# Attention heads of the last two batches spread in one stream over the mixture's second and third batch of columns and seven output tiles

## The chip, the cores and the metric

One core of a Trainium2 chip runs the whole program. The metric is device time in microseconds (us), the median of three runs. TensorE does the matmuls and transposes, VectorE (DVE), ScalarE (ACT) and GpSimd (POOL) do the elementwise work, SyncE (SP) issues the DMA transfers.

## The reference

Attention over 4 batches, 12 heads, 448 positions and 64 channels feeds a mixture of three products with a maximum over them, and that feeds eight experts of which each token takes one:

```python
scores = scale * np.matmul(q, k.transpose(0, 1, 3, 2))
scores = np.where(mask, -1000000000.0, scores)      # causal
attn = exp(scores - max); attn /= sum
x = np.matmul(attn, v)                              # (1792, 768) once the heads stand side by side
h = np.maximum(np.maximum(x @ w1, x @ w2), x @ w3)  # (1792, 768)
y = h @ w_out                                       # (1792, 768)
e_idx = np.argmax(y @ w_gate, axis=1)
...
out[mask] = gate_w * eom * (np.maximum(y[mask] @ e_w1[e], 0) @ e_w2[e])
```

## The kernel before

A unit u is a pair of heads of one batch: 24 units, six for each batch, so batch 2 is units 12 to 17 and batch 3 units 18 to 23. Units 0 to 11 are worked in an order written out by hand, beside the mixture of batch 0. From there on the order is made by three generators and by `mix` (L806), and each engine takes its instructions in that order nearly as they are written.

- `attn_stream` (L564) yields the work of units 12 to 23 in 85 steps, seven to a unit: scores (`at_qk`, L433: 24 matmuls into six PSUM banks, named ss), two steps of transposes of the other head of the unit before (`at_p`, L497: three banks pp, 10 transposes), its product with v (`at_av`, L525: 8 matmuls into av) with the transposes pr of the row sums, the transposes of this unit's first head in two steps, the second with the transposes pq and pk of the next unit's q and k (`at_t`, L407), and the product av of the first head. ps_t (L96) has six PSUM banks, which all of these share with the transposes pwt of w_out. VectorE takes scores out of their banks with one instruction for each block (L466), ScalarE does the exponentials (L471).
- `h_stream(b)` (L691) yields the mixture of batch b in 36 halves of 9 matmuls (L674). Two halves make one product in one bank pm of the two banks of psm (L85). `h_max` (L678) copies the first of three products to g on ScalarE, takes the maximum with the second and third on VectorE (L685), and writes hth (ScalarE, L688) and htl (VectorE, L689). The weights wp come back from memory in 384 KB pieces, five tiles ahead (L657).
- `y_half(t, a)` (L707) yields one half of the columns of output tile t in two steps of 9 matmuls (L713) into a psm bank py, and ends with a copy ys (ScalarE, L722). Tiles 0 to 6 read the hth and htl of batches 0 and 1, so they stand after `h_stream(1)`; `h_stream(2)` writes over batch 0's place in them, so it stands after tile 6.
- `wo_stream` (L207) unpacks w_out beside `h_stream(1)` in 12 pieces: ScalarE L159 and L160, VectorE L165 to L167 and GpSimd L170 make a piece wor, ScalarE and GpSimd split it, TensorE transposes it (pwt, L194), and for each second piece TensorE multiplies it with the gates (pg, L200: 6 matmuls in the program, two passes of each in the trace, into a psm bank).
- `x_split(hp)` (L612) writes the parts xh (ScalarE, L615) and xl (L617, VectorE for odd hp, GpSimd for even) of the finished heads xf. There is one buffer each of xf, xh and xl for a pair of heads, so the split of batch 2 must come after the last half of `h_stream(1)` that reads batch 1's, and batch 3's heads write xf only after that split.

`mix` walks one generator and after each of its steps adds `ratio` to a counter that stands for head steps, at most 1.0 of which is carried:

```python
for _ in st:
    next(beside, None)
    acc[0] += ratio
    while acc[0] >= 1.0 and not all(u in done for u in range(NN, upto)):
        next(ast, None)
        acc[0] -= 1.0
    acc[0] = min(acc[0], 1.0)
```

Before, 36 halves of `h_stream(1)` take 1.33 head steps each, which is 47 steps and finishes batch 2; all six splits follow; the 28 steps of tiles 0 to 6 take 1.75 each, so the last 38 steps of heads are used up before tile 6; `h_stream(2)` (L830) then runs with nothing beside it. After it come the splits of batch 3, tiles 7 to 9, the routing, `h_stream(3)` and the experts.

Of the kernel before, what the change touches and what calls it, by code (L numbers as in the profile page):

```python
# [23 lines left out]
def f32(ap):  # L24
    return ap.bitcast(F32)
# [7 lines left out]
def kernel(  # L33
# [18 lines left out]
    NP = H // 2  # L52
# [17 lines left out]


    G_PRIO = 300
    RATIO = (1.33, 1.75)
    WB = 5
    DA, SA = 6, 3

# [3 lines left out]
    def prio(n):  # L80
        return tc.high_priority(offset=n)
# [34 lines left out]
    def wo_tiles(dt, name):  # L116
        for a in "hl":
            wo[a] = wo_p.tile([P, KF, DM + 2 * E], dt, tag="wo" + a, name=name + a)
# [12 lines left out]
    def drain(g):  # L131
        for _ in g:
            pass
# [4 lines left out]
    def decode_load(src, n=0):  # L138
        n = n % 6
        if n < 2:  # L140
            raw = dec.tile([P, 2 * HC], I32, tag="raw", name="raw")
        else:
            raw = wo["h"][:, n - 2, : 2 * HC]
        raw = raw.rearrange("p (n t) -> p n t", t=2)
        if len(src.shape) == 2:
            dst = raw.rearrange("p n t -> p (n t)")
        else:
            dst = raw.rearrange("p (k n) t -> p k (n t)", k=src.shape[1])
        nc.sync.dma_start(out=dst, in_=src)
        return raw  # L150

    def decode_act(raw, n=0):
        lo, hi = raw[:, :, 0], raw[:, :, 1]
        if n % 3:
            tlf = wo["l"][:, n % 3 - 1, : 2 * HC]
        else:
            tlf = dec.tile([P, 2 * HC], I32, tag="tlf", name="tlf", bufs=1)
        t, lf = tlf[:, :HC].bitcast(F32), tlf[:, HC : 2 * HC]
        nc.scalar.activation(t, hi.bitcast(F32), AF.Abs, scale=65536.0)  # L159
        nc.scalar.activation(lf, lo.bitcast(U32), AF.Copy, scale=2.0**-29)  # L160
        return t, lf

    def decode_steps(dst, raw, t, lf):
        hi, ti = raw[:, :, 1], t.bitcast(I32)
        yield nc.vector.tensor_scalar(out=t, in0=t, scalar1=LO, scalar2=HI, op0=ALU.max, op1=ALU.min)  # L165
        yield nc.vector.tensor_single_scalar(ti, ti, 3, op=ALU.logical_shift_left)
        yield nc.vector.scalar_tensor_tensor(  # L167
            out=ti, in0=hi, scalar=-0x80000000, in1=ti, op0=ALU.bitwise_and, op1=ALU.bitwise_or
        )
        nc.gpsimd.tensor_tensor(out=dst.bitcast(I32), in0=ti, in1=lf, op=ALU.add)  # L170
# [12 lines left out]
    def wo_src(f, a):  # L183
        return w_out[f * P : (f + 1) * P, 2 * HC * a : 2 * HC * (a + 1)]

    def wo_split(f, a, wr):
        yc = slice(HNL * a, HNL * a + HN)
        nc.scalar.copy(wo["h"][:, f, yc], wr)
        nc.gpsimd.tensor_sub(wo["l"][:, f, yc], wr, f32(wo["h"][:, f, yc]))

    def wo_t(f, a, wr, wt):
        pt = ps_t.tile([P, 512], F32, tag="pst", name=f"pwt{f}_{a}")
        for c in range(3):
            nc.tensor.transpose(pt[:, c * P : (c + 1) * P], wr[:, c * P : (c + 1) * P], ident)  # L194
        nc.vector.tensor_copy(wt[:, 3 * a : 3 * a + 3, :], pt[:, : 3 * P])

    def wo_g(f, wt):
        pg = psm.tile([P, 512], F32, tag="mm", name=f"pg{f}")
        for dk in range(KD):
            nc.tensor.matmul(  # L200
                pg[:, : 2 * E], lhsT=wt[:, dk, :], rhs=wg[:, dk].rearrange("p a e -> p (a e)"),
                start=dk == 0, stop=dk == KD - 1,
            )
        nc.scalar.copy(wo["h"][:, f, HN:HNL], pg[:, : 2 * E])
        nc.vector.tensor_sub(wo["l"][:, f, HN:HNL], pg[:, : 2 * E], f32(wo["h"][:, f, HN:HNL]))

    def wo_stream():  # L207
        wo_tiles(F32R, "wo")
        raw = decode_load(wo_src(0, 0))
        for n in range(2 * KF):  # L210
            f, a = divmod(n, 2)
            if a == 0:
                wt = dec.tile([P, KD, P], F32, tag="wt", name=f"wt{f}", bufs=1)
            wr = dec.tile([P, HC], F32, tag="wraw", name=f"wor{n}", bufs=3)
            steps = decode_steps(wr, raw, *decode_act(raw))
            if n + 1 < 2 * KF:
                raw = decode_load(wo_src(*divmod(n + 1, 2)))
            drain(steps)
            yield
            wo_split(f, a, wr)  # L220
            wo_t(f, a, wr, wt)
            yield
            if a:
                wo_g(f, wt)
                yield
# [6 lines left out]
    NN, NU = 2 * NP, B * NP  # L232
    raws, done = {}, set()
# [378 lines left out]
    def x_split(hp):  # L612
        xh = xtp.tile([P, S], F32R, tag=f"xh{hp}", name=f"xh{hp}")
        xl = xtp.tile([P, S], F32R, tag=f"xl{hp}", name=f"xl{hp}")
        nc.scalar.copy(xh, xf[hp])  # L615
        eng = nc.vector if hp % 2 else nc.gpsimd
        eng.tensor_sub(xl, xf[hp], f32(xh))  # L617
        xs[hp] = (xh, xl)
# [38 lines left out]
    def ahead(n):  # L657
        while fetched[0] < min(n, len(seq)):
            b, i, a = seq[fetched[0]]
            wp = wst.tile([P, 2, 3, P], F32R, tag="wp", name=f"wp{b}_{i}_{a}", bufs=WB)  # L660
            nc.sync.dma_start(out=f32(wp).rearrange("p a k n -> p (a k n)"), in_=wpdram[2 * i + a])
            wtiles[b, i, a] = wp
            fetched[0] += 1
# [3 lines left out]
    def h_half(b, i, a):  # L667
        pm = gs["pm", b, i] = gs.get(("pm", b, i)) or psm.tile([P, 512], F32, tag="mm", name=f"pm{b}_{i}")
        wp = wtiles.pop((b, i, a))
        for kk in range(3 * a, 3 * a + 3):  # L670
            xh, xl = xs[kk]
            wh, wl = wp[:, 0], wp[:, 1]
            for c, (l, r) in enumerate(((wh, xh), (wh, xl), (wl, xh))):
                nc.tensor.matmul(  # L674
                    pm[:, :S], lhsT=l[:, kk % 3, :], rhs=r, start=kk == 0 and c == 0, stop=kk == KD - 1 and c == 2
                )
# [14 lines left out]
    def h_stream(b):  # L691
        for i in range(NCH):
            n = NH * (b - 1) + 2 * i
            ahead(n + WB)
            h_half(b, i, 0)
            ahead(n + 1 + WB)
            yield
            h_half(b, i, 1)
            with prio(G_PRIO):
                h_max(b, i)  # L700
            yield


    def y_cols(t):
        return slice(P * (t % 7), P * (t % 7) + P)

    def y_half(t, a):  # L707
        cs = y_cols(t)
        c0, w = (0, HNL) if a == 0 else (HNL, HN)
        pm = psm.tile([P, 512], F32, tag="mm", name=f"py{t}_{a}")  # L710
        for kk in range(KF):
            for c, (l, r) in enumerate(((hth, wo["h"]), (htl, wo["h"]), (hth, wo["l"]))):
                nc.tensor.matmul(  # L713
                    pm[:, :w], lhsT=l[:, kk, cs], rhs=r[:, kk, c0 : c0 + w], start=kk == 0 and c == 0,
                    stop=kk == KF - 1 and c == 2,
                )
            if kk == 2:
                yield
        if a == 0:
            nc.vector.tensor_copy(lg[:, t].rearrange("p a e -> p (a e)"), pm[:, HN:HNL])  # L720
        ys = ysp.tile([P, HN], F32, tag="ys", name=f"ys{t}_{a}")
        nc.scalar.copy(ys, pm[:, :HN])  # L722
        nc.sync.dma_start(out=ydram[t * P : (t + 1) * P, HN * a : HN * a + HN], in_=ys)
        yield
# [81 lines left out]
    def mix(st, upto, ratio, beside=iter(()), acc=[0.0]):  # L806
# [8 lines that stand above are left out]
    def rest(upto):  # L815
        while not all(u in done for u in range(NN, upto)):
            next(ast)

    wos = wo_stream()
    mix(h_stream(1), NP * 3, RATIO[0], wos)  # L820
    rest(NP * 3)
    for hp in range(NP):
        x_split(hp)
    drain(wos)
    for t in range(7):
        for a in range(2):
            mix(y_half(t, a), NU, RATIO[1])
    rest(NU)
    ph_a.close()
    for _ in h_stream(2):  # L830
        pass
    for hp in range(NP):
        x_split(hp)
    for t in range(7, 10):
# [153 lines left out]
    rest = rt.tile([P, E], F32, name="rest")  # L988
# [343 lines left out]
```

## Time and profile before

| | |
|---|---|
| median of 3 runs | 963.58 us (962.23 to 967.49) |
| the profiled execution | 967.17 us, of which 965.4 us are the span from its first to its last instruction |
| TensorE busy | 931.5 us, 96% of the span |
| VectorE, ScalarE, GpSimd busy | 484.1, 456.1 and 167.3 us |
| chain of work that ended last | TensorE 80%, VectorE 8%, ScalarE 5%, issue 3%, DMA 3% |

The profile is one execution. A matmul's busy time overlaps that of the next, so TensorE's progress is read from start to start, and its losses from the idle time that the trace puts before an instruction together with what ended it. PEld is TensorE's weight load, which runs beside the matmuls. In the rows, SPq is the queue of SyncE.

### The profile page before, as it was taken

Reading aid. Unit: us, or ns where it says so; the run is one execution under the profiler, and the core shown is the slowest. Engines: PE = TensorE matmul, PEld = TensorE weight load, DVE = VectorE, ACT = ScalarE, POOL = GpSimd, SP = SyncE. Lnnn points to the kernel's source line nnn. Section 1 sums busy time; section 2 is a strip of 40 time slices with the busy share of each in tenths; the row PEclk is TensorE's granted clock in tenths of the full one; section 3 lists DMA queues with packets and bytes.
Section 4 is the critical chain, followed back from the end, with each engine's and each line's share of the span. In section 5 each row is a group of like instructions: output and inputs, shape, how many; then the busy total and the mean of one; then the engine's idle time right before and its main releaser. Section 6 shows DMA issues by size and latency. Waiting matters only on the chain.

```text
span 965.4 us, 17091 instructions
## 1 busy us (share of the span) xinstructions
PE 931.5 (96%) x5500; PEld 825.5 (86%) x5500; DVE 484.1 (50%) x1287; ACT 456.1 (47%) x1037; POOL 167.3 (17%) x186
## 2 busy tenths in 40 slices
PE   8888999999999999999999999899999999999997
PEld 5666888888889989989999899888998998998996
DVE  4665777867776666662124313641211217749244
ACT  5876676655666567761012013142212216757253
POOL 0114555542221121010001000010010010100101
PEclk9998999999999999999999999999999999999999
DMA  6436878876564542204772994181111016939410
GB/s 144 101 92 200 250 247 242 255 241 186 154 167 128 144 131 68 59 26 147 218 213 86 329 332 125 52 325 54 34 44 56 34 38 228 357 128 370 155 34 26
DMA packets 126354, 150.10 MB, mean 155 GB/s; under 512 B 75934, under 2 KB 93342, under 8 KB 126240
## 3 DMA queue, kind: packets, MB, share of 16 engines
q1 hardware_dynamic: 123200, 135.37, 44.8%
q0 software_dynamic: 3040, 13.41, 4.0%
q8 instruction: 46, 0.75, 0.3%
q14 instruction: 68, 0.56, 0.2%
HBM read 129.85 MB, written 26.77 MB: 162 GB/s over the span
## 4 chain that ended last, share of the span: by engine, by line
PE 80%; DVE 8%; ACT 5%; issue 3%; DMA 3%; POOL 1%; SPq 0%; POOLq 0%; ACTq 0%; DVEq 0%
PE pm L674 23%; PE po L1226 15%; PE ph L1207 15%; PE py L713 7%; PE ss L452 3%; PE pp L511 2%; PE av L547 2%; PE an L332 2%; PE av L535 2%; PE pht L1218 2%; ACT pt L471 1%; PE pxt L1143 1%; PE sn L284 1%; DVE pt L466 1%; PE pn L312 1%
## 5 line engine op out<-in xcount | busy, mean ns | idle before, releaser
L674 PE MATMUL pm<-xh,wp 128*128 128x448 f32 x864 | 265.8, 375 | 0.2 <-DMA wp<-wpdram 0.2
L674 PEld LDWEIGHTS pm<-xh,wp 128*128 128x128 f32 x864 | 162.9, 189 | 22.7 <-issue 9.8
L674 PE MATMUL pm<-xl,wp 128*128 128x448 f32 x432 | 158.8, 367 | 0.0
L1226 PE MATMUL po<-w2h,th 128*128 128x384 f32 x288 | 100.2, 348 | 0.0
L1226 PE MATMUL po<-w2l,th 128*128 128x384 f32 x288 | 97.1, 337 | 0.0
L1226 PE MATMUL po<-w2h,tl 128*128 128x384 f32 x288 | 97.0, 337 | 0.0
L1221 DVE TENSOR_TENSOR tl<-pht,th 128x512 fp32r<-128x512 f32 x36 | 24.8, 689 | 135.2 <-ACT th L1220 88.5
L471 ACT ACTIVATE pt<-pt,bm 112x224 f32<-112x224 f32 (+3 forms) x144 | 74.8, 521 | 28.2 <-DVE bm L466 27.2
L674 PEld LDWEIGHTS pm<-xl,wp 128*128 128x128 f32 x432 | 81.8, 189 | 5.8 <-issue 0.3
L1207 PE MATMUL ph<-w1h,xh 128*128 128x512 f32 x216 | 86.4, 400 | 0.0
L1207 PE MATMUL ph<-w1h,xl 128*128 128x512 f32 x216 | 85.1, 394 | 0.2 <-DVE xl L1146 0.2
L1207 PE MATMUL ph<-w1l,xh 128*128 128x512 f32 x216 | 84.7, 392 | 0.0
L685 DVE TENSOR_TENSOR g<-pm,g 128x448 f32<-128x448 f32 x48 | 29.8, 621 | 101.2 <-PE pm L674 100.7
L1235 POOL DMA_INDIRECT out_dram<-os,six x18 | 18.4, 1020 | 283.7 <-ACT os L1234 171.2
L713 PE MATMUL py<-woh,hth 128*128 128x400 f32 (+1 forms) x168 | 60.1, 358 | 3.6 <-ACT ys L722 3.6
L466 DVE CUSTOM_DVE_ANT_0 pt<-ss,mask 112x224 f32<-112x224 f32 (+3 forms) x144 | 57.7, 443 | 6.2 <-PE ss L452 6.1
L688 ACT CAST hth<-g 128x448 fp32r<-128x448 f32 x24 | 13.6, 567 | 99.2 <-DVE g L685 99.2
L713 PE MATMUL py<-wol,hth 128*128 128x400 f32 (+1 forms) x168 | 58.1, 346 | 0.0
L713 PE MATMUL py<-woh,htl 128*128 128x400 f32 (+1 forms) x168 | 58.0, 345 | 0.0
L1226 PEld LDWEIGHTS po<-w2h,tl 128*128 128x128 f32 x288 | 54.2, 188 | 0.8
L1212 ACT ACTIVATE h__7114<-ph 128x512 f32<-128x512 f32 x36 | 21.6, 599 | 70.2 <-PE ph L1207 70.2
L1226 PEld LDWEIGHTS po<-w2h,th 128*128 128x128 f32 x288 | 54.1, 188 | 0.7
(273 smaller groups left out, 1847.0 us busy)
## 6 DMA issues: line engine op xcount, KB each, us to landing
wp<-wpdram SPq DMA_DIRECT2D x108, 384.0 KB
w1r<-in_moe_w_dram SPq DMA_DIRECT2D x42, 512.0 KB
w2r<-in_moe_w_dram SPq DMA_DIRECT2D x56, 384.0 KB
wpdram<-wp SPq DMA_DIRECT2D x36, 384.0 KB
wxh<-in_moe_w_dram SPq DMA_DIRECT2D x24, 384.0 KB
qraw<-in_q_dram SPq DMA_DIRECT2D x48, 112.0 KB
kraw<-in_k_dram SPq DMA_DIRECT2D x48, 112.0 KB
vraw<-in_v_dram SPq DMA_DIRECT2D x48, 112.0 KB
```

The lines of the kernel that those rows point to most:

```text
L332: nc.tensor.matmul(av4[:, i, j], lhsT=n_pth[u, j][:, o : o + CP], rhs=v_[:, kt, j], start=kt == 0, stop=kt == b)
L452: nc.tensor.matmul(ss, lhsT=l[m, qc], rhs=r[m, :L], start=n == 0, stop=n == len(prods) - 1)
L466: nc.vector.tensor_tensor_reduce(out=pr, in0=ss, in1=mask[:, S - L :], scale=1.0, scalar=3.0e38, op0=ALU.add, op1=ALU.min, accum_out=bm[:, ...
L471: nc.scalar.activation(pr, pr, AF.Exp, bias=bm[:, i : i + 1], scale=-1.0, accum_out=sm[:, j, i : i + 1])
L511: nc.tensor.transpose(pp[:CP, off : off + CP], pt[:, POFF[i] + kt * CP : POFF[i] + (kt + 1) * CP], ident[:CP, :CP])
L674: nc.tensor.matmul(pm[:, :S], lhsT=l[:, kk % 3, :], rhs=r, start=kk == 0 and c == 0, stop=kk == KD - 1 and c == 2)
L685: nc.vector.tensor_max(gs["g"], pm[:, :S], gs["g"])
L713: nc.tensor.matmul(pm[:, :w], lhsT=l[:, kk, cs], rhs=r[:, kk, c0 : c0 + w], start=kk == 0 and c == 0, stop=kk == KF - 1 and c == 2,)
L1207: nc.tensor.matmul(pm[a], lhsT=l[:, kk], rhs=r[kk][:, cs], start=kk == 0 and c == 0, stop=kk == KD - 1 and c == 2)
L1212: nc.scalar.activation(h_[:, 512 * a : 512 * a + 512], pm[a], AF.Relu)
L1221: nc.vector.tensor_sub(tl[:, kr], pt, f32(th[:, kr]))
L1226: nc.tensor.matmul(po[a][:, :HN], lhsT=l[:, kk], rhs=r[kk][:, HN * a : HN * a + HN], start=kk == 0 and c == 0, stop=kk == KF2 - 1 and c == 2,)
```

## The change

One ratio, 0.92, stands for both. `h_stream(1)` mixes in 33 head steps, the 28 steps of tiles 0 to 6 mix in 25, and `h_stream(2)` is mixed with the 27 that are left, over its first 29 halves. Batch 2 is split as its pairs of heads come to their end, looked for after each `y_half`; batch 3 still after `h_stream(2)`. The memory of the head stage is given back (`ph_a.close()`) after `h_stream(2)`, where it was given back before it.

```diff
@@ -70,7 +70,7 @@
 
 
     G_PRIO = 300
-    RATIO = (1.33, 1.75)
+    RATIO = 0.92
     WB = 5
     DA, SA = 6, 3
 
@@ -816,19 +816,28 @@
         while not all(u in done for u in range(NN, upto)):
             next(ast)
 
+
+
     wos = wo_stream()
-    mix(h_stream(1), NP * 3, RATIO[0], wos)
-    rest(NP * 3)
-    for hp in range(NP):
-        x_split(hp)
+    mix(h_stream(1), NU, RATIO, wos)
     drain(wos)
+    split = []
+
+    def split_done():
+        for hp in range(NP):
+            if hp not in split and 2 * NP + hp in done:
+                x_split(hp)
+                split.append(hp)
+
     for t in range(7):
         for a in range(2):
-            mix(y_half(t, a), NU, RATIO[1])
+            mix(y_half(t, a), NU, RATIO)
+            split_done()
+    rest(NP * 3)
+    split_done()
+    mix(h_stream(2), NU, RATIO)
     rest(NU)
     ph_a.close()
-    for _ in h_stream(2):
-        pass
     for hp in range(NP):
         x_split(hp)
     for t in range(7, 10):
```

TensorE, in the mixture of batch 1, at the scores of unit 13 (ss13; the number behind the name's last underscore is the buffer's). Before, the end of the scores and what follows:

```order
L452 MATMUL ss13_0_3_2816<-kl13_2716,qh13_2713 112x448
L452 MATMUL ss13_1_3_2817<-kl13_2716,qh13_2713 112x448
L511 MATMUL pp12_1_0_2837<-ident_89,pt12_1_2635 112x112 x4
L511 MATMUL pp12_1_1_2844<-ident_89,pt12_1_2635 112x112 x4
L674 MATMUL pm1_3_2775<-xh3_2465,wp1_3_1_2623 128x448
L674 MATMUL pm1_3_2775<-xl3_2466,wp1_3_1_2623 128x448
L674 MATMUL pm1_3_2775<-xh3_2465,wp1_3_1_2623 128x448
L674 MATMUL pm1_3_2775<-xh4_2474,wp1_3_1_2623 128x448
L674 MATMUL pm1_3_2775<-xl4_2475,wp1_3_1_2623 128x448
```

With the change:

```order
L452 MATMUL ss13_1_3_2859<-kl13_2760,qh13_2757 112x448
L674 MATMUL pm1_4_2817<-xh3_2465,wp1_4_1_2674 128x448
L674 MATMUL pm1_4_2817<-xl3_2466,wp1_4_1_2674 128x448
L674 MATMUL pm1_4_2817<-xh3_2465,wp1_4_1_2674 128x448
L674 MATMUL pm1_4_2817<-xh4_2474,wp1_4_1_2674 128x448
L674 MATMUL pm1_4_2817<-xl4_2475,wp1_4_1_2674 128x448
L674 MATMUL pm1_4_2817<-xh4_2474,wp1_4_1_2674 128x448
L674 MATMUL pm1_4_2817<-xh5_2483,wp1_4_1_2674 128x448
L674 MATMUL pm1_4_2817<-xl5_2484,wp1_4_1_2674 128x448
L674 MATMUL pm1_4_2817<-xh5_2483,wp1_4_1_2674 128x448
L200 MATMUL pg1_2887<-wg_104,wt1_2704 128x16 x6
L511 MATMUL pp12_1_0_2898<-ident_89,pt12_1_2652 112x112 x4
```

The transposes pp12_1 stood right behind the scores; nine matmuls of the mixture and the gates' product pg1 stand between now.

TensorE, in w_out's product, at the scores of unit 19. Before:

```order
L547 MATMUL av18_0_4350<-pth18_0_4291,vs18_4227 128x112
L547 MATMUL av18_0_4350<-ptl18_0_4292,vs18_4227 128x112
L547 MATMUL av18_0_4350<-pth18_0_4291,vs18_4227 128x224
L547 MATMUL av18_0_4350<-ptl18_0_4292,vs18_4227 128x224
L452 MATMUL ss19_0_0_4362<-kh19_4314,qh19_4312 112x112
L452 MATMUL ss19_1_0_4363<-kh19_4314,qh19_4312 112x112
L452 MATMUL ss19_0_0_4362<-kh19_4314,ql19_4313 112x112
```

With the change:

```order
L547 MATMUL av18_0_4530<-pth18_0_4457,vs18_4427 128x224
L547 MATMUL av18_0_4530<-ptl18_0_4458,vs18_4427 128x224
L713 MATMUL py4_1_4542<-woh_2514,hth_101 128x384
L713 MATMUL py4_1_4542<-woh_2514,htl_102 128x384
L713 MATMUL py4_1_4542<-wol_2515,hth_101 128x384
L713 MATMUL py4_1_4542<-woh_2514,hth_101 128x384
L713 MATMUL py4_1_4542<-woh_2514,htl_102 128x384
L713 MATMUL py4_1_4542<-wol_2515,hth_101 128x384
L713 MATMUL py4_1_4542<-woh_2514,hth_101 128x384
L713 MATMUL py4_1_4542<-woh_2514,htl_102 128x384
L713 MATMUL py4_1_4542<-wol_2515,hth_101 128x384
L452 MATMUL ss19_0_0_4552<-kh19_4494,qh19_4492 112x112
```

The scores stood right behind the product with v of unit 18's first head; nine matmuls of an output tile stand between now.

ScalarE, where the mixture of batch 1 passes into w_out's product, with the change (xh is `x_split`'s cast, pt an exponential, mn and rb belong to the end of unit 15, vs to v of unit 16):

```order
L522 CAST pth15_1_3840<-pp15_1_2_3866 112x224
L615 CAST xh0_4005<-xf12_2802 128x448
L471 ACTIVATE pt16_1_3871,sm16_3817<-pt16_1_3871,bm16_1_3872 112x112
L471 ACTIVATE pt16_1_3871,sm16_3817<-pt16_1_3871,bm16_1_3872 112x224
L471 ACTIVATE pt16_1_3871,sm16_3817<-pt16_1_3871,bm16_1_3872 112x336
L615 CAST xh1_4009<-xf13_3132 128x448
L471 ACTIVATE pt16_1_3871,sm16_3817<-pt16_1_3871,bm16_1_3872 112x448
L615 CAST xh2_4013<-xf14_3442 128x448
L552 COPY mn15_1_3904<-av15_1_3895 64x448
L403 CAST vs16_3907<-vraw16_3653 112x4x64 x2
L479 COPY rb16_3923<-sm16_3817 112x512
L615 CAST xh3_4017<-xf15_3761 128x448
```

Before, all six casts xh stood here, between the exponentials of unit 18; four stand here now, between those of unit 16, and the casts xh4 and xh5 stand later, each behind the end of its unit.

## Rows read from the trace of the kernel before

**Rows 1.** Stretches of the run, in us from its start: length, then busy time of each engine:

```profile
core 0: us, PE busy (x) PEld busy (x) DVE busy (x) ACT busy (x) POOL busy (x), PEclk, DMA share, GB/s
216.00:349.80 133.80, 128.41 (x904) 115.51 (x903) 91.82 (x258) 85.49 (x240) 27.96 (x30) 1.00 0.55 156
349.80:434.00 84.20, 82.53 (x608) 76.28 (x607) 54.20 (x166) 59.91 (x171) 10.03 (x13) 1.00 0.21 59
434.00:442.00 8.00, 8.00 (x47) 8.00 (x46) 3.72 (x19) 0.96 (x2) 1.72 (x11) 1.00 0.14 49
442.00:505.00 63.00, 63.00 (x313) 58.39 (x312) 10.00 (x16) 6.64 (x13) 0.00 (x0) 1.00 0.70 209
```

**Rows 2.** TensorE's waits from 216 to 450 us: us in total, times, longest:

```profile
PE pp L511 <- DVE bm L466: 4.0, 3, 2.7
PE ss L452 <- DVE xf L553: 0.9, 2, 0.5
PE av L547 <- DVE ptl L523: 0.8, 1, 0.8
PE av L547 <- POOL vs L404: 0.7, 1, 0.7
PE ss L452 <- DVE kl L431: 0.4, 2, 0.2
```

**Rows 3.** Order of time around 240 us: start, length, instruction, [idle before it]:

```profile
237.49 0.49 PE L194 MATMUL pwt<-ident,wor 128*128 128x128 f32 x3
...
238.12 1.02 POOL L170 TENSOR_TENSOR wor<-tlf 128x384 int32<-128x384 int32 x1 [6.17 <-PE pwt L194]
...
239.47 0.37 PE L452 MATMUL ss<-kl,qh 64*112 64x448 f32 x2
...
240.23 0.74 DVE L165 TENSOR_SCALAR tlf<-tlf 128x384 f32<-128x384 f32 x1 [1.66 <-ACT tlf L159]
...
241.88 0.27 DVE L466 CUSTOM_DVE_ANT_0 pt<-ss,mask 112x112 f32<-112x112 f32 x1
...
242.52 1.02 PE L511 MATMUL pp<-ident,pt 112*112 112x112 f32 x8 [2.69 <-DVE bm L466]
...
243.35 0.08 DVE L466 DVE_READ_ACCUMULATOR2_ANT bm<- 112x1 f32 x1
```

**Rows 4.** Order of time on TensorE, at unit 14's scores:

```profile
262.69 0.37 PE L674 MATMUL pm<-xl,wp 128*128 128x448 f32 x1
262.89 0.36 PE L674 MATMUL pm<-xh,wp 128*128 128x448 f32 x1
263.86 1.38 PE L511 MATMUL pp<-ident,pt 112*112 112x112 f32 x10 [0.61 <-DVE bm L466]
```

**Rows 5.** Order of time on TensorE, w_out's product, end of unit 20's scores:

```profile
372.75 0.84 PE L452 MATMUL ss<-kh,qh 64*112 64x448 f32 x2
373.14 0.65 PE L452 MATMUL ss<-kh,ql 64*112 64x448 f32 x2
...
373.93 0.44 PE L713 MATMUL py<-woh,hth 128*128 128x384 f32 x1
...
375.61 1.12 PE L511 MATMUL pp<-ident,pt 112*112 112x112 f32 x10
```

**Rows 6.** Groups by line, 217 to 442 us: count | busy us, mean ns | idle before:

```profile
L685 DVE TENSOR_TENSOR g<-pm,g 128x448 f32<-128x448 f32 x12 | 7.4, 621 | 3.8 <-PE pm L674 3.7
...
L615 ACT CAST xh<-xf 128x448 fp32r<-128x448 f32 x6 | 3.2, 563 | 0.1
...
L617 POOL TENSOR_TENSOR xl<-xf,xh 128x448 fp32r<-128x448 f32 x3 | 3.8, 1262 | 14.1 <-ACT xh L615 14.1
...
L617 DVE TENSOR_TENSOR xl<-xf,xh 128x448 fp32r<-128x448 f32 x3 | 2.7, 923 | 0.0
```

**Rows 7.** Waits of SyncE's queue, 216 to 442 us:

```profile
SPq L661 <- PE pm L674: 34.4, 15, 5.2
```

**Rows 8.** Order of time on TensorE, a product with v behind the transposes:

```profile
288.47 0.44 PE L547 MATMUL av<-pth,vs 112*128 112x448 f32 x1 [0.75 <-DVE ptl L523]
```

## The prediction

> **What bounds the kernel now.** I read the busy time by stretches first, since the page's shares mix stages. The change touches 216 to 505 us: the mixture of batch 1 with heads (to 349.8), w_out's product with heads (to 434) and without (to 442), the mixture of batch 2 with nothing beside it (to 505) [rows 1]. The reader should see three things there. TensorE is the engine that sets the end: VectorE and ScalarE are busy for 69% and 64% of the first stretch and for 64% and 71% of the second. TensorE is idle for 133.8 - 128.41 = 5.39 us in the first stretch, for 84.2 - 82.53 = 1.67 us in the second, and not at all from 434 us on: 7.06 us together. And the granted clock is 1.00 of full speed, 2.4 GHz, in all of them, also where the engine has just stood still for 2.69 us, so a gap costs itself and no slower matmuls after it.
>
> The list of TensorE's waits says which work was late: 4.0 us in 3 waits for VectorE to take scores out of their banks (bm), 0.9 in 2 for VectorE's xf, 0.8 and 0.7 in one each for ptl and vs ahead of a product with v, 0.4 in 2 for kl [rows 2]. None is for a DMA.
>
> The order in time shows how the largest comes about [rows 3]. w_out's transposes pwt start at 237.49 and free a buffer wor, for which GpSimd had waited; its L170 runs at 238.12, ScalarE follows, then VectorE's three unpacking instructions from 240.23. VectorE takes unit 13's scores only behind these, at 241.88, though TensorE had issued the last of them at 239.47. The scores fill all six banks of ps_t, so the transposes pp wait for the first to come free: 2.69 us. Unit 14 has nine matmuls between scores and transposes, 1.8 us of cover, and still waits 0.61 [rows 4].
>
> Idle time understates the loss, since a matmul's modelled end lies behind the start of a follower. On unit 14 the start-to-start time is 263.86 - 262.89 = 0.97 us where 262.89 - 262.69 = 0.20 is usual: 0.77 lost, 0.61 shown, 0.16 hidden [rows 4]. In w_out's product the scores follow straight on the product with v that holds the last bank, and the last pair of score matmuls takes 373.14 - 372.75 = 0.39 us for 0.20, a loss of 0.19 that shows as nearly no idle time [rows 5]. There are four such beside the nine listed waits. So the loss is about 7.06 + 13 x 0.16 = **9.1 us**, and that is all that a change of order alone can win here.
>
> **The change, part by part.**
>
> *TensorE's own work* stays: the same matmuls and transposes in another order. I cost the finer interleaving at nothing; every step of heads already stood between blocks of nine.
>
> *Fewer heads beside the mixture of batch 1* (33 steps for 47). Unit 13: behind its scores now come nine matmuls, 9 x 0.20 = 1.8 us, and pg; so the transposes come at least 1.8 us later, against a wait of 2.69 + 0.16, and pg's twelve passes are longer than the remaining one microsecond if they take the 0.1 us that the transposes take (pp: 1.02 us for 8, less the tail of the last) [rows 3]. The wait goes. What is late next is VectorE's maximum of the product that ended behind the scores: VectorE ends unit 13's first four score instructions at 243.35 + 0.08, 1.55 us after 241.88 [rows 3], and then needs 0.62 for the maximum [rows 6], while TensorE reaches the next product with pg holding the other psm bank. I put 0.4 us there. Unit 14 keeps its pattern (pwt, scores, nine matmuls, pp): 0.77 stays. Unit 15 has eighteen matmuls and pg in between, unit 16 no unpacking ahead of it: nothing. The wait for unit 12's kl at the start keeps its four matmuls of cover: about 0.4 stays.
>
> *w_out's product* (25 steps for 38). Nine matmuls, 1.68 us [rows 5], stand between the product with v and the next scores: the two listed waits for xf and the four small ones go, and so does the second kl. One product with v waited 0.75 us for ptl with two transposes ahead of it [rows 8]; nine matmuls part them now, except in the last unit, where I leave 0.4 us, between nothing and 0.75 + 0.16.
>
> *The mixture of batch 2* takes 27 steps. Heads there find VectorE with 10.0 us of work in 63.0 [rows 1] and no unpacking of w_out. From 349.8 to 442 us a head step costs (92.2 - 1.67 - 28 x 1.68)/38 = 1.15 us of TensorE, an estimate, so a half takes 1.8 + 0.92 x 1.15 = 2.9 us and the stretch grows by what the two before it shrink. I put no wait there.
>
> *Splits and waits that are moved.* Six casts of 0.56 us on ScalarE, three subtractions of 1.26 on GpSimd, three of 0.92 on VectorE [rows 6], as before, but the cast xh0 now waits, among unit 16's exponentials, for the half of the mixture that still reads the old xh0. Queued behind it on ScalarE are the rest of unit 16's exponentials, mn, vs and the first pth of unit 16; TensorE wants the last of these, behind two banks of transposes, three blocks of w_out's product and unit 17's q and k, some 7 us later, and ScalarE's queue is about as long. Costed at nothing; without that cover it would be one wait of 1 us. The constants of the routing, 3.72 us of VectorE and 1.72 of GpSimd [rows 1], now run beside the last seven halves of batch 2's mixture, off TensorE's path.
>
> *Transfers.* SyncE issues q, k and v for three units between the weight pieces of batch 2. It waits 34.4 us for TensorE to free weight tiles, in 15 waits [rows 7]: it is ahead. Four halves of 2.9 us lie between the fetch and the use. Costed at nothing.
>
> *From tile 7 on* the order on every engine is the same.
>
> **Sum:** 9.1 lost now; 0.4 + 0.4 + 0.77 + 0.4 = 2.0 stay. The gain is 7.1 us, which takes the profiled execution from 967.2 to 960.1 and the median, 3.6 us below it, from 963.58 to **956.5 us**.
>
> **A rule weighed.** The row on unit 13 shows the transposes stopped by six full banks, while in w_out's product the same six banks are refilled and the transposes follow nine matmuls later at 375.61 with no idle time [rows 5]; so the late VectorE, not the number of banks, makes the wait. The Trainium skill, Perfetto Trace Analysis, section Optimization Strategy, says of bubbles that repeat that they "can mean there isn't enough SBUF/PSUM for the next tile to be allocated", which would call for more banks and not for more room between the steps. By that rule the waits would come back at each unit's scores; that is the first rival below.
>
> **The rivals.**
> 1. *The banks stay the limit.* Units 13, 15 and 16 and the three score blocks in batch 2's mixture each keep a wait like unit 14's, 6 x 0.77 = 4.6 us: gain 9.1 - 2.0 - 4.6 = 2.5, 961.1 us. For it: unit 14 waited despite its nine matmuls. Against it: the waits came only where unpacking stood ahead on VectorE. 0.22.
> 2. *VectorE is late for the maximum in batch 2's mixture*, and the time is slower. psm has two banks, so the maximum of one product must be done when the product after the next begins, 2 x 2.9 = 5.8 us later. Two blocks of scores, 1.55 each, and the maximum, 0.62, take 3.7: the slack is 2.1 us. It decides from there on; if VectorE came 3.1 us late, 1 us beyond it at each of 14 products, it would cost 14 us: 963.6 - 7.1 + 14 = 970.5 us. Against it: no matmul of the mixture waits in [rows 2], where heads are denser. 0.06.
> 3. *More is won*, since the four leftovers are covered as well: 9.1 us, 954.5. 0.07.
>
> **How the numbers follow.** The forecast has 0.65. The runs before lie from 1.4 us under their median to 3.9 over it, and half a per cent, 4.8 us, is about what a measurement of this kernel can tell from no change. Faster by more than that means under 958.8 us: the forecast's case but for its edge (0.61) and the third rival, 0.68. Within it: that edge and nearly all of the first rival, 0.26. Slower by more: the second rival, 0.06. The range goes from 953.5 (9.1 us won, and a run 1 us low) to 961.5 (the first rival's 961.1).
>
> **What would show it.** In the changed profile: TensorE's idle time between 216 us and the end of batch 2's mixture at about 1 to 2 us for 7.06; the waits for bm down to one, at unit 14; none for xf; that stretch about 7 us shorter; the mixture of batch 2 at about 5.8 us for each product until its fifteenth; the stretch behind it as before. It would be wrong if waits for bm or for the maximum appeared at every unit, if weight matmuls waited for a DMA, or if the idle time went and the time did not.

## The result, and the profile after

The changed kernel takes **957.38 us** (median of 6 runs, 955.4 to 959.22), the kernel before beside it 965.72 (median of 6). The ratio is 0.9904, 95% interval 0.9883 to 0.9925: 7.2 to 11.3 us faster. The forecast was 956.5 in a range of 953.5 to 961.5.

The profiled execution took 959.22 us, with a span of 957.5. I measure the stretch that the change touches from the start of the last px transpose to the start of the first matmul of tile 7: from 216.79 to 507.71 us before, from 217.83 to 499.64 after, 290.92 against 281.81. That is 9.1 us. From there to the end it is 457.7 and 457.8 us. So the whole gain lies in the stretch.

Busy time by stretches of the kernel after; the mixture of batch 1, w_out's product, and the mixture of batch 2 with heads and without:

```profile
core 0: us, PE busy (x) PEld busy (x) DVE busy (x) ACT busy (x) POOL busy (x), PEclk, DMA share, GB/s
217.00:331.00 114.00, 112.59 (x760) 102.10 (x759) 73.90 (x201) 66.15 (x183) 24.70 (x26) 1.00 0.59 170
331.00:404.00 73.00, 73.00 (x524) 69.79 (x523) 37.73 (x114) 43.77 (x122) 7.13 (x10) 1.00 0.29 79
404.00:477.00 73.00, 73.00 (x476) 66.46 (x475) 40.59 (x114) 40.52 (x113) 5.75 (x8) 1.00 0.52 151
477.00:499.50 22.50, 22.50 (x126) 20.73 (x124) 10.84 (x31) 7.22 (x16) 3.75 (x13) 1.00 0.52 162
```

TensorE is idle for 114.00 - 112.59 = 1.41 us, where it was 7.06 [rows 1], and not at all from 331 us on. VectorE's load is now even, 52% and 56% in the second and third stretch, where it was 64% and 16%. The waits of TensorE that are left, from 216 to 505 us:

```profile
PE pp L511 <- DVE bm L466: 0.6, 1, 0.6
PE pg L200 <- DVE g L685: 0.4, 1, 0.4
PE ss L452 <- DVE kl L431: 0.2, 1, 0.2
```

Against [rows 2], two of three waits for bm, both for xf, the one for ptl and the one for vs are gone, and one for the maximum g is new. Unit 13, where 2.69 us stood [rows 3], in time order on TensorE:

```profile
245.28 0.37 PE L452 MATMUL ss<-kl,qh 64*112 64x448 f32 x2
245.58 0.47 PE L674 MATMUL pm<-xh,wp 128*128 128x448 f32 x1
...
247.51 1.41 PE L200 MATMUL pg<-wg,wt 128*128 128x16 f32 x12
248.77 0.96 PE L511 MATMUL pp<-ident,pt 112*112 112x112 f32 x8
249.86 0.47 PE L674 MATMUL pm<-xh,wp 128*128 128x448 f32 x1
```

Nine matmuls and pg stand between scores and transposes, and the transposes start without a wait. What is late instead, by less, is the mixture behind them: its first weight load waits for VectorE's maximum.

```profile
249.86 0.19 PEld L674 LDWEIGHTS pm<-xh,wp 128*128 128x128 f32 x1 [0.35 <-DVE g L685]
```

At unit 14 the wait has stayed, as in [rows 4]:

```profile
273.51 0.37 PE L674 MATMUL pm<-xh,wp 128*128 128x448 f32 x1
274.52 0.73 PE L511 MATMUL pp<-ident,pt 112*112 112x112 f32 x5 [0.65 <-DVE bm L466]
```

In w_out's product the end of a unit's scores, to be held against [rows 5], now looks like this:

```profile
380.76 0.36 PE L452 MATMUL ss<-kh,qh 64*112 64x448 f32 x2
380.96 0.36 PE L452 MATMUL ss<-kh,ql 64*112 64x448 f32 x2
381.16 0.37 PE L452 MATMUL ss<-kl,qh 64*112 64x448 f32 x2
381.46 0.44 PE L713 MATMUL py<-woh,hth 128*128 128x384 f32 x1
```

A row x2 is the pair of two heads. The first row of the last six matmuls was 0.84 us long and is 0.36; from its start to the product that follows it is 0.70 us, where it was 373.93 - 372.75 = 1.18.

### The profile page after: what moved, and what is told of

It reads as the page before. It is cut to its first block, busy times and chain, and to the rows that moved or that the text cites. A ratio compares the mean times of both kernels' runs of the same rounds, so it can differ in the third digit from the quotient of the medians.

```text
span 957.5 us, 17073 instructions
## 1 busy us (share of the span) xinstructions
PE 929.2 (97%) x5500; PEld 825.3 (86%) x5500; DVE 486.0 (51%) x1287; ACT 458.1 (48%) x1037; POOL 166.9 (17%) x186
## 4 chain that ended last, share of the span: by engine, by line
PE 85%; DVE 8%; ACT 4%; issue 1%; DMA 1%; POOL 1%; SPq 0%; POOLq 0%; ACTq 0%; DVEq 0%
PE pm L674 24%; PE po L1235 16%; PE ph L1216 16%; PE py L713 9%; PE ss L452 3%; PE pp L511 3%; PE av L547 3%; PE av L535 2%; PE an L332 2%; PE pht L1227 2%; DVE pt L466 1%; PE pxt L1152 1%; ACT pt L471 1%; PE sn L284 1%; PE pr L486 1%
## 5 line engine op out<-in xcount | busy, mean ns | idle before, releaser
L674 PE MATMUL pm<-xh,wp 128*128 128x448 f32 x864 | 272.0, 378 | 0.1
L1235 PEld LDWEIGHTS po<-w2l,th 128*128 128x128 f32 x288 | 54.0, 188 | 0.0
```

What stands on the lines that cost most here:

```text
L674: nc.tensor.matmul(pm[:, :S], lhsT=l[:, kk % 3, :], rhs=r, start=kk == 0 and c == 0, stop=kk == KD - 1 and c == 2)
L1235: nc.tensor.matmul(po[a][:, :HN], lhsT=l[:, kk], rhs=r[kk][:, HN * a : HN * a + HN], start=kk == 0 and c == 0, stop=kk == KF2 - 1 and c == 2,)
```

## The experiments

My theory was that the gain is the waits that went, at two places: (a) transposes that wait for full banks in batch 1's mixture, because VectorE has w_out's unpacking ahead of the scores; (b) scores that stand directly behind the product with v in w_out's product and wait for its bank. The rivals: the heads beside batch 2's mixture are the gain by themselves, since VectorE stood idle there; or the split of x head by head is.

In all that follows "the stretch" is the one measured above, with its three stages (batch 1 from the start of the stretch, the others from first matmul to first matmul). The ratios are to the kernel before.

| kernel | stretch, us | batch 1 | w_out's product | batch 2 | ratio (95%) |
|---|---|---|---|---|---|
| before | 290.9 | 133.0 | 92.3 | 65.7 | 1 |
| changed | 281.8 | 113.8 | 72.6 | 95.4 | 0.9904 (0.9883 to 0.9925) |
| x split together | 281.8 | 113.8 | 72.6 | 95.4 | 0.986 (0.9833 to 0.9887) |
| heads thinned in batch 1 alone | 287.5 | 113.7 | 104.7 | 69.1 | 0.9962 (0.9947 to 0.9976) |
| heads thinned in w_out's product alone | 288.8 | 135.5 | 72.6 | 80.7 | 0.9947 (0.9923 to 0.9972) |
| before, heads ahead of unpacking | 286.3 | 128.3 | 92.3 | 65.7 | 0.9937 (0.9914 to 0.9959) |
| before, finer openings | 288.4 | 133.1 | 89.7 | 65.7 | 0.9963 (0.9946 to 0.9981) |
| before, both orders | 283.8 | 128.5 | 89.7 | 65.7 | 0.9904 (0.9873 to 0.9935) |
| changed, heads ahead of unpacking | 280.7 | 112.7 | 72.6 | 95.4 | 0.9893 (0.9856 to 0.993) |
| the same, `parts1` spread | 280.8 | 112.8 | 72.6 | 95.4 | 0.9817 (0.9792 to 0.9843) |

**The split of x.**

```diff
     def split_done():
+        if split or not all(2 * NP + hp in done for hp in range(NP)):
+            return
         for hp in range(NP):
-            if hp not in split and 2 * NP + hp in done:
-                x_split(hp)
-                split.append(hp)
+            x_split(hp)
+            split.append(hp)
```

> The changed kernel, but the six splits of x for batch 2 stand together behind the last of its heads, as they did before, and no longer one behind each pair of heads. My theory (the gain is TensorE's waits that went: for full banks ahead of the transposes in batch 1's mixture, and at scores that stand directly behind the product with v in w_out's product): as the changed kernel within 1 us, 956 to 959 us, a ratio of 0.990 to before. Rival (the gain is the head-by-head split, which has xh and xl of batch 2 ready earlier): the mixture of batch 2 then waits for the splits, six casts of 0.56 us on ScalarE and three subtractions of 1.26 us on GpSimd in a row, 3 to 5 us, ratio 0.993 to 0.996, and a wait of TensorE for xh or xl shows at the first product of batch 2.

955.3 us. All three stages are those of the changed kernel, and no wait for xh or xl shows. Splitting head by head is worth nothing in the stretch. The ratio came out lower than I expected, with an interval that touches the changed kernel's; the stretch does not hold the reason, and it stays open.

**The two halves of the change.** One table of ratios, two settings (the second has 1.33 and 0.92):

```diff
-    mix(h_stream(1), NU, RATIO, wos)
+    mix(h_stream(1), NU, 0.92, wos)
...
+    def mix_y(st, acc=[0.0]):
+        for _ in st:
+            acc[0] += 1.86
...
-            mix(y_half(t, a), NU, RATIO)
+            mix_y(y_half(t, a))
...
-    mix(h_stream(2), NU, RATIO)
+    mix(h_stream(2), NU, 0.92)
```

> The changed kernel with the heads thinned in the mixture of batch 1 alone: 0.92 of a head step for each half there, 1.86 steps for each block of nine in w_out's product so that all heads end in it, and nothing beside the mixture of batch 2. My theory: in the mixture of batch 1 TensorE loses about 1.3 us as in the changed kernel, and the waits for xf and ptl of w_out's product come back, some 7 to 9 score blocks with 0.5 us each, 4 to 5 us in all: 961 to 963 us, ratio 0.994 to 0.996. Rival (the gain is the heads beside batch 2's mixture, whose VectorE and ScalarE stood idle before): the gain goes altogether, ratio 0.999 to 1.001.

> The other half of the change: 1.33 head steps for each half of batch 1's mixture as before, 0.92 in w_out's product, the rest in the mixture of batch 2. My theory: the waits for full banks ahead of the transposes of units 13 to 15 come back with some 2.9, 0.8 and 0.8 us, 5 us in all with ptl, and no wait for xf in w_out's product: 961 to 963 us, ratio 0.994 to 0.996. Rival (heads beside batch 2's mixture are the gain): as the changed kernel, ratio 0.990.

964.07 and 963.93 us: each half alone gives a part, and both intervals leave the rivals out. The first keeps the changed kernel's 113.7 us in batch 1, the second its 72.6 in w_out's product. But in the first the waits that I expected did not come: none for xf is listed in w_out's product, and three score blocks take 1.83 to 1.92 us for 1.57, 0.9 us in all. The products with v wait instead (0.8 us for vs, 0.4 for ptl, 0.3 for pth); from start to start they take 3.7 us more than in the changed kernel. So this run shows that the density costs time, not that it costs it at the scores.

In the second, the ratio is the expected one and the waits for bm are back, 4.0 us in three, but batch 1's mixture is 2.5 us longer than in the kernel before. 0.8 of it are eight transposes pp, which stand in it and no longer in w_out's product. For most of the rest the trace of this one execution has the reason: behind the wait of unit 13, the granted clock fell.

```profile
236.00:242.00 6.00, 3.38 (x33) 2.66 (x32) 3.39 (x11) 1.68 (x5) 2.03 (x2) 1.00 0.61 205
243.00:246.00 3.00, 3.00 (x11) 2.64 (x10) 1.25 (x2) 1.87 (x6) 0.00 (x0) 0.54 0.34 121
247.00:250.00 3.00, 3.00 (x21) 2.80 (x20) 2.63 (x9) 2.29 (x9) 0.96 (x1) 1.00 0.57 154
```

The same in time order on TensorE:

```profile
242.08 1.02 PE L511 MATMUL pp<-ident,pt 112*112 112x112 f32 x8 [2.70 <-DVE bm L466]
242.87 0.45 PE L674 MATMUL pm<-xh,wp 128*128 128x448 f32 x1
...
244.59 0.95 PE L674 MATMUL pm<-xh,wp 128*128 128x448 f32 x2
245.34 0.58 PE L674 MATMUL pm<-xl,wp 128*128 128x448 f32 x1
```

After 2.70 us of standing still most of 243 to 246 us runs at 0.5 of full speed, 1.2 GHz; seven matmuls are followed by the next after 0.37 us instead of 0.20, and with those at either end about 1.5 us are lost.

**Cause (a) by itself.** The kernel before with one line moved, no head less beside batch 1's mixture:

```diff
         for _ in st:
-            next(beside, None)
             acc[0] += ratio
...
             acc[0] = min(acc[0], 1.0)
+            next(beside, None)
```

> The kernel before, its density of heads untouched, with one line moved: in each half of batch 1's mixture the step of heads is written ahead of w_out's unpacking step and not behind it, so VectorE takes a unit's scores before the three unpacking instructions. My theory: the wait of 2.69 us of unit 13's transposes falls to under 1 us and those of units 14 and 15 (0.61, 0.68) to about nothing: 3 to 4.5 us faster, ratio 0.9955 to 0.997, with the stretch of w_out's product unchanged. Rival (the density of the heads itself fills the banks): the three waits stay within 1 us in all, ratio 0.999 to 1.001.

961.77 us. Batch 1's mixture shrinks by 4.7 us, and the other two stages are as before. The moved line puts every engine's part of the unpacking behind the heads, TensorE's pwt too. Unit 13 in time order on TensorE, now without a matmul between its scores and its transposes, and VectorE's first instruction for these scores:

```profile
235.97 0.37 PE L452 MATMUL ss<-kl,qh 64*112 64x448 f32 x2
236.27 0.98 PE L511 MATMUL pp<-ident,pt 112*112 112x112 f32 x8
```

```profile
235.30 0.28 DVE L466 CUSTOM_DVE_ANT_0 pt<-ss,mask 112x112 f32<-112x112 f32 x1 [1.34 <-PE ss L452]
```

The 2.69 us are gone with the same six banks and the same density. VectorE took the first score at 235.30, while TensorE was still at the last ones; before, it came to them at 241.88, 2.41 us behind the start of TensorE's last [rows 3]. Not all went as I had it: at unit 14 the pwt, which now stand behind the scores, wait 0.6 us for bm in place of the transposes. And 0.5 of the 4.7 us came at unit 16, whose scores take 1.85 us for 2.37.

**Cause (b) by itself.** The kernel before with openings after six matmuls instead of nine, and as many head steps in all:

```diff
-    RATIO = (1.33, 1.75)
+    RATIO = (1.33, 1.75 * 2 / 3)
+    FINE = (1, 3)
...
-            if kk == 2:
+            if kk in FINE:
```

> The kernel before with as many head steps in w_out's product as before, but blocks of six matmuls between the openings and not of nine, with 1.17 steps for each: scores then mostly no longer stand directly behind the product with v. Batch 1's mixture is as before and nothing stands beside batch 2's. My theory: score blocks in w_out's product fall to 1.57 us, and that stretch from 92.3 us to 88 to 90: 2.5 to 4 us faster, ratio 0.996 to 0.9975. Rival (what counts is how many head steps share the stretch, so that only moving them to batch 2's mixture helps): the stretch stays within 1 us of 92.3, ratio 0.999 to 1.001.

964.35 us. All score blocks in w_out's product take 1.57 us from first to last start; before they took 2.94, 2.04, 2.11, 2.04 and 2.11. That is 3.4 us, and the stage shrank by 2.6. The difference is a wait that the kernel before did not have: with six matmuls instead of nine ahead of it, one product with v comes before its ptl is there.

```profile
355.10 0.47 PE L548 MATMUL av<-ptl,vs 112*128 112x448 f32 x1 [0.87 <-DVE ptl L524]
```

From start to start it costs 1.0 us; the wait for vs shrank by 0.2. 3.4 - 1.0 + 0.2 = 2.6, so the added openings themselves cost nothing that can be seen.

**Both orders, no head moved to batch 2.**

> The kernel before with both changes of order that were tried apart: the step of heads ahead of w_out's unpacking in batch 1's mixture, and openings after six matmuls in w_out's product. Heads stay where they were, none beside batch 2's mixture. My theory (late releases at two places are the gain, not where the heads lie): the two gains of the stretch from the last px to tile 7, 4.7 and 2.5 us, add: 283 to 284.5 us for 290.9, against 281.8 in the changed kernel; ratio 0.991 to 0.994. Rival (a good part of the gain needs heads beside batch 2's mixture): the stretch stays above 285.5 us.

959.71 us. The parts add: 133.0 - 128.5 and 92.3 - 89.7 make 7.1 of the 9.1 us, and nothing stands beside batch 2's mixture. In the stretch the rival falls but for the rest of 2.0 us; the ratio alone, 0.9904, is the changed kernel's and cannot tell the two apart. The waits left in this kernel say where most of the rest may lie:

```profile
PE av L548 <- DVE ptl L524: 1.7, 3, 0.9
PE pwt L195 <- DVE bm L467: 0.6, 1, 0.6
PE av L548 <- POOL vs L405: 0.5, 1, 0.5
PE ss L453 <- DVE kl L432: 0.2, 1, 0.2
```

The products with v still stand close behind their transposes, 2.2 us of waiting, of which 0.9 is the wait that the finer openings brought; in the changed kernel nine matmuls part them, and none of these waits is listed. That the 2.0 us are these waits was not tried by itself.

**What a late bank costs.** Two heads' score matmuls start in pairs, 3 to 4 ns apart, and a pair takes as long as one. I thought that a wait in the middle of a pair costs more than itself, because the pairs fall out of step. Three kernels, one run each, were to show it: the matmuls of the two heads written one head after the other, in the changed kernel and in the one before, and the last two banks taken in the other order.

```diff
-            for n, (l, r) in enumerate(prods):
+            for m, ss in sl if u >= NN else ():
+                for n, (l, r) in enumerate(prods):
+                    nc.tensor.matmul(ss, lhsT=l[m, qc], rhs=r[m, :L], start=n == 0, stop=n == len(prods) - 1)
+            for n, (l, r) in enumerate(prods) if u < NN else ():
                 for m, ss in sl:
                     nc.tensor.matmul(ss, lhsT=l[m, qc], rhs=r[m, :L], start=n == 0, stop=n == len(prods) - 1)
```

```diff
-            for j in range(2):
+            for j in (1, 0) if i == 3 and u >= NN else (0, 1):
...
+            sl = sl[::-1] if i == 3 and u >= NN else sl
```

> The changed kernel with the 24 score matmuls of a unit written one head after the other for batches 1 and 2, and not in pairs of the two heads. My theory says that the block of scores is short because the two heads of a pair run side by side, and that the kernel before lost about 0.5 us at each block where a wait stood inside a pair: from the first to the last start a block then takes some 3.0 us for 1.57, twelve blocks, 15 to 18 us slower than the changed kernel: about 973 us. Rival (matmuls of two heads do not share time, and the longer blocks of before were only waits): the blocks stay within 0.2 us of 1.57 and the time within 2 us of the changed kernel.

> The kernel before, with the score matmuls of batches 1 and 2 written one head after the other. In the changed kernel this made no difference, since the two heads' matmuls still ran side by side, three places apart. My theory (in w_out's product a wait for xf inside the last bank's matmuls costs the pairs that fall out of step, not the wait alone): the wait now stands at the fourth of the last six matmuls, so that five slots of 0.2 us are needed there and no longer four: the blocks of units 20 to 23 go from 2.04 to 2.11 us (first to last start) to 2.2 to 2.35, while blocks without a wait stay at 1.57. Rival (only the time of the release counts): they stay at 2.0 to 2.1.

> The kernel before, in which the last two banks of a unit's scores are only taken in the other order, so that the wait for xf falls on the first matmul of a pair of heads and not on its second. My theory (a wait inside a pair puts the rest of the block out of step, about 0.5 us for a wait that shows as 0.02 to 0.08): the five blocks in w_out's product that took 2.04 to 2.94 us from first to last start take 1.57 plus the wait itself, 1.6 to 1.9, and the stretch from the last px to tile 7 shrinks by 1.5 to 2.5 us. Rival (the blocks are long because the wait is long): they stay at 2.0 to 2.1 and the stretch within 0.5 us of 290.9.

All three came out against me: 958.33, 963.54 and 964.09 us, and the blocks kept their length to 0.03 us. The blocks are the evidence here, since a single run cannot settle a microsecond. The last edit settles nothing: one matmul of the pair still started on time and the other 0.39 us behind it. The other two are clear. In the changed kernel, written one head after the other, time order on TensorE:

```profile
243.64 0.38 PE L452 MATMUL ss<-kh,qh 64*112 64x448 f32 x2
243.85 0.37 PE L452 MATMUL ss<-kh,ql 64*112 64x448 f32 x2
244.05 0.37 PE L452 MATMUL ss<-kl,qh 64*112 64x448 f32 x2
```

A block of one head has one kh,qh, so the x2 is both heads: the second head's, written fourth, starts with the first head's, ahead of the two written before it. The rival of this edit had the blocks right, but not for its own reason: the two heads do share time. And in the kernel before, written so, with the wait:

```profile
370.08 0.37 PE L452 MATMUL ss<-kh,qh 64*112 64x448 f32 x1
370.29 0.36 PE L452 MATMUL ss<-kh,ql 64*112 64x448 f32 x1
370.47 0.45 PE L452 MATMUL ss<-kh,qh 64*112 64x448 f32 x1
370.49 0.36 PE L452 MATMUL ss<-kl,qh 64*112 64x448 f32 x1
370.76 0.35 PE L452 MATMUL ss<-kh,ql 64*112 64x448 f32 x1
370.96 0.36 PE L452 MATMUL ss<-kl,qh 64*112 64x448 f32 x1
```

The first head goes on alone while the second waits for its bank until 370.47, 0.39 us behind the first, as in [rows 5]; then its three matmuls follow, the first slot 0.29 us long for 0.20. What the first head does meanwhile saves nothing, for it would have run beside the second anyway. So the loss is the full lateness of the bank and the slow start, 0.39 + 0.1 = 0.5 us; for the same block in the kernel before, the profile shows 0.02 of it as idle time. The rival that only the time of the release counts was right.

**What is left.** The changed kernel with the line of cause (a) moved as well, and then with the six steps `parts1` spread, each of which copies a piece of the first expert's weights on ScalarE (w1h) and subtracts on VectorE (w1l):

```diff
-    for i in range(KD):
-        parts1(i)
     for t in range(TL, NTT):
         drain(y_half(t, 0))
+        for i in {TL + 1: (0, 1), TL + 2: (2, 3), TL + 3: (4, 5)}.get(t, ()):
+            parts1(i)
```

> The changed kernel with w_out's unpacking step written behind the step of heads in each half of batch 1's mixture. My theory: unit 14's transposes, which still wait 0.65 us, wait less than 0.2, and the stretch from the last px to tile 7 shrinks by 0.5 to 1.2 us from 281.8: a ratio to before within 0.002 of the changed kernel's. Rival (the wait comes from the density of heads, not from the unpacking ahead on VectorE): unit 14's wait stays at 0.6.

> The sixth experiment's kernel, and beside it w_out's product of tiles 10 to 13 written ahead of most of ScalarE's six copies of the first expert's weights. In the changed kernel TensorE waits 3.6 us for a ys copy that stands behind these copies. My theory: that wait falls to under 1.5 us and the kernel is 2 to 4 us faster than the changed one, a ratio of 0.985 to 0.989. Rival (the first expert is then late by as much, since its weights are copied later): the wait moves to the expert's first matmuls and the ratio stays at 0.989 to 0.992.

956.65 and 948.93 us. Unit 14's wait went, but 0.6 us of pwt's, behind unit 15's scores, took its place, so the stretch shrank by 1.1 and the ratio cannot be told from the changed kernel's. The second edit beats both kernels: 1.8% under the one before, with an interval that lies below the changed kernel's. In the changed kernel these were the wait and what came behind it, first the wait:

```profile
PE py L713 <- ACT ys L722: 3.6, 1, 3.6
```

The copy ys was late, but not behind ScalarE's copies, as I had expected: these end at 595.29, and ScalarE then has one more pair of casts and stands idle for 1.57 us. VectorE was late. Its six subtractions w1l stand ahead of lg, the copy of the gates' columns out of the same bank, and lg is what the profile names as ending the idle time before ys:

```profile
590.58 6.90 DVE L1160 TENSOR_TENSOR w1l<-w1r,w1h 128x1024 fp32r<-128x1024 f32 x6 [1.24 <-ACT w1h L1159]
597.40 0.25 DVE L720 COPY lg<-py 128x16 f32<-128x16 f32 x2
597.60 0.86 ACT L722 COPY ys<-py 128x384 f32<-128x384 f32 x2 [1.57 <-DVE lg L720]
```

The edit spreads both, so it helps all the same. The stretches around the wait:

```profile
594.50:598.10 3.60, 0.03 (x1) 0.00 (x0) 3.60 (x7) 2.03 (x5) 0.00 (x0) 0.82 0.00 0
598.10:603.00 4.90, 4.87 (x15) 4.82 (x16) 0.48 (x2) 0.36 (x1) 0.00 (x0) 0.50 0.22 80
```

And the kernel with the steps spread, in the same place:

```profile
585.00:619.00 34.00, 34.00 (x194) 31.66 (x193) 25.61 (x107) 14.61 (x24) 0.00 (x0) 1.00 0.26 87
```

3.6 us of standing still and then 4.9 us at a granted clock of 0.50 are gone; from tile 10's first matmul to the first expert's first it is 28.1 us, where it was 34.7, and the expert takes hardly longer (336.2 us to the end for 335.5, and 336.2 in the kernel before). The rival, that the expert would come late by as much, falls.

## Why the prediction was right, and where a term was off

*What bounds.* Right: TensorE in all stages, and the gain is the time that it lost. The granted clock is 1.00 in all four stretches after.

*Unit 13.* Its wait went. What I had put next, VectorE's maximum, was late: the mixture behind pp starts at 249.86, 0.39 us after the last pp where 0.03 is usual, so 0.37 us late for 0.4 forecast.

*Unit 14.* 274.52 - 273.51 = 1.01 for 0.20: 0.81 lost, where 0.77 was to stay. *kl:* 0.48 for 0.4. *The last unit's product with v:* nothing, for 0.4. A wait of pg for g near 231 us, 0.57, was not foreseen. The sum of what stays is 2.2 us, and I had 2.0.

*The mis-sized term* is the one of what was lost before: "There are four such beside the nine listed waits", each "a loss of 0.19 that shows as nearly no idle time". I compared the pair that waits with the usual 0.20 and stopped there. Such a block takes 2.04 to 2.11 us for 1.57, a loss of 0.5; and unit 16's block and unit 19's (2.37 and 2.94) lose 0.8 and 1.4, more than their listed waits with 0.16 each. Over these six blocks that is 13.6 - 6 x 1.57 = 4.2 us, where my terms had 0.9 + 0.2 for the listed xf and kl, 3 x 0.16 and 4 x 0.19, 2.3 in all. So some 11 us were lost and not 9.1; less 2.2 that is 8.8, and 9.1 was measured. By the medians the gain is 965.72 - 957.38 = 8.3 us; the time came out 0.9 us above the forecast since the kernel before ran 2.1 us above the 963.58 from which the forecast was made. The gain was 1.2 us more than the 7.1 forecast, so the two misses partly cancel: that the time is so close is in part luck.

*Interleaving costed at nothing* was right as far as it can be seen. An entry into the mixture costs 0.08 us (0.29 from the first matmul behind transposes to the next, for 0.20), and there are 62 of them where 37 were, which would be 2 us. But what was lost before less what stays makes 8.8 us, and 9.1 were gained, and in the finer openings above nothing is left over for the openings either. I take it that steps which stood together had paid as much among themselves; no run shows that by itself.

*The splits, the transfers, the constants:* no wait of TensorE for any of them. From tile 7 on 457.8 us for 457.7.

*The rule weighed, and rival 1.* Moving one line took 2.69 us of waiting for a bank to nothing, with six banks as before. The Trainium skill, Perfetto Trace Analysis, section Optimization Strategy, says that bubbles that repeat can mean too little SBUF or PSUM for the next tile. Here they did not: the bank was the thing waited for and a late engine the cause. The same section says that where the most contended engine changes over time, interleaving those regimes may help. Here TensorE was the fullest in every stage, so that case is not this one; and 7.1 of the 9.1 us came from two changes of order alone, with nothing moved beside batch 2's mixture, so at most the other 2.0 are owed to the move.

*Rival 2* (VectorE late for batch 2's maximum): no wait shows in that mixture. *Rival 3* (9.1 us won): the number was reached, by another way; the leftovers stayed, and more had been lost.

## What to carry to other kernels

Where a full buffer stops the bounding engine, look at what stands ahead of the release on the engine that frees it; one line of order was worth 4.7 us with the buffers as they were. Measure a loss from start to start over the whole group and against a group that runs freely, since a wait under cover of a twin that runs beside costs its full length and shows as nearly no idle time. And put other work between the matmuls that fill a bank and the next ones that need it back; how much is a matter of measuring, since six matmuls instead of nine took away one kind of wait here and brought back another, of 0.87 us.

## What the runs showed of the chip that was not expected

Matmuls of 64 rows in two halves of the array start out of the order in which they were written: the fourth together with the first, 0.2 us ahead of the second. With the bank late, the second started 0.18 us ahead of the fourth, so no one fixed order fits both. The Trainium skill, TensorE: Matmul & The Clock Gate, section The mechanism, has matmuls strictly first in, first out; these two traces do not agree for two halves.

A standstill of about 2.7 us was followed by a granted clock of 0.5 or not: after 2.69 us it stayed at 1.00 in the kernel before, and in the three other profiled executions with unit 13's wait at 2.65 to 2.70; after 2.70 in the kernel with batch 1 dense it was 0.54 for 3 us. My sentence that a gap costs itself and no slower matmuls held for the profiled execution only.

Where nothing disturbs them, the mixture's matmuls run in one of two spacings. The same undisturbed part of batch 2, from 488 to 499 us, by shape, after and then before:

```profile
L674 PE MATMUL pm<-xh,wp 128*128 128x448 f32 x37 | 10.7, 368 | 0.0
```

```profile
L674 PE MATMUL pm<-xh,wp 128*128 128x448 f32 x37 | 10.6, 365 | 0.0
```

From start to start it is 206.7 ns after and 202.7 before, at a granted clock of 1.00 in both. Over 300 matmuls that is 1.2 us. It changes within one execution (in the changed kernel it goes back to 202.7 at 551 us), and what sets it stays open.
